# Phases summed in turns in the first four slabs, sixteen more mask matmuls, the last product in two steps, and a new order of the work

## The chip, the core and the metric

The kernel runs on one core of one Trainium2 chip. The metric is device time of one execution in microseconds (us); the time of a kernel is the median of its runs. Engines are named as in the profile: PE multiplies matrices, DVE and ACT do the elementwise work, POOL does next to nothing here, SP starts the DMAs (SPq and ACTq are the queues of SP and ACT).

## What is computed

A linear attention whose state decays by a complex factor, and a gated feed-forward network on its output:

```python
mag = sqrt(a_re**2 + a_im**2)
scale = minimum(mag, 0.999) / (mag + 1e-6)
a_re, a_im = a_re * scale, a_im * scale
for t in range(S):                        # S = 768, for each of B*H = 4*8, D = 48
    S_re, S_im = a_re[t] * S_re - a_im[t] * S_im, a_re[t] * S_im + a_im[t] * S_re
    S_re += k[t] (x) v[t]
    y[t] = q[t] @ S_re
x = y as [3072 tokens, 384]
out = (silu(x @ w_gate) * (x @ w_val)) @ w_out      # 384 -> 1536 -> 384
```

The kernel doesn't step through t. In chunks of 128 rows it sums the logs of the decay's size and its phases from the chunk's first row on, which turns the recurrence into a masked product of q and k with their phases and sizes multiplied in, plus a state that is carried from chunk to chunk.

## The kernel before

**Tiles.** A slab is 128 tokens of one of the four sequences, 8 heads of 48 columns, so 128 by 384. Two slabs make a group g, twelve groups in all; c is the chunk in the sequence that a group belongs to (groups 0 and 1 have c = 0, groups 2 and 3 c = 1, and so on). Group 1 and all later ones treat both slabs in one instruction where they can (128 by 768). Group 0 is the first work of the kernel and is cut in two halves, 0a and 0b, of one slab each.

**Stage of a group** (`stage_ops`). From a_re and a_im come the log of the size (`lnr r0 sqr sqi m2 l2 lnm w`: Ln, Exp, squares) and the phase (`ratio at`: an Arctan). Both are summed over the rows of a chunk by a matmul with the triangular mask `tri`: `cumL` for the log, `cumF` for the phase, one matmul per slab (L545 for groups 0 and 1; L548, with operands in two parts, for later groups). `exps` (L560, L561) takes the exponentials of cumL's sums straight from PSUM. The sums of the phase go through three steps before their cosine and sine are taken:

- `sadd` (L605 to L609) takes the sum from PSUM to SBUF, times 1/(2 pi) (L607), and for c > 0 adds what the chunk before left over (L609, one scalar_tensor_tensor). One instruction per slab.
- `rnd` (L616) rounds that to whole turns, by adding a large constant and taking it away. One instruction per stage.
- `frac` (the helper on L404) subtracts the whole turns. One instruction per stage. What it leaves in the chunk's last row is also stored (`fr`) for the next chunk.

`abs`, `cos` and `sin` (ACT, L453) follow, and the products of q and k with them (`qs0 qs1 ks0 ks1`, DVE, L404).

**Slabs and network.** `slab_ops` transposes (`tr`, L673 for the first four slabs), multiplies q with k (`sc`, L734), masks (`mk`, L762), multiplies with v (`V`, L734), updates the state (`kv`, L800/L803) and copies the result out (`evh`, L821). `ffn_ops` runs twelve blocks f of the hidden width per group: `f1` (L982, both input products), `th` (silu, ACT, L988), `h2` (product, DVE, L993), `hh` and `hl` (high and low part, L408/L410 and L404), `f2` (L1013, the output product, summed over the blocks in PSUM). Then `oe` copies the sums out (L408/L410) and `os` stores them (L1028), in three pieces per group. In group 0 the first four blocks use whole weights and the others weights in two parts; the weights are rounded and split by `c1` to `c5` on DVE and ACT early in the kernel (L873, L408, L410).

**Warm-up and end.** `wm` (L1086) are 48 matmuls of the mask with itself whose result nobody uses; a row of the trace counts each as two passes. `judge`, `tally` (L1040 to L1048) and `keep` (L1052) count how many inputs lie outside the range that this quick way is exact for; after the stores each engine loads the count (L1261) and branches on it (L1262) past `general()`, a slower way that isn't taken with these inputs.

**What sets the order.** The string `ORDER` (L36 on) is the whole order: names of steps, with the engine where there is a choice (`sqi1:ACT`). The planner walks it, puts each step behind the others of its engine, and each engine works its queue in order; a step waits for its operands and for its buffer to come free. Table changes of ACT (L1118) are put in where two neighbours need different tables. DMAs are issued by SP in the same order.

Of the kernel before, what the change touches and what calls it, by code (L numbers as in the profile page):

```python
# [22 lines left out]
P = 128  # L23
# [13 lines left out]
    wm0 wm1 wm2 wm3 wm4 wm5 wm6 wm7 wm8 wm9 wm10 wm11 wm12 wm13 wm14 wm15 wm16 wm17 wm18 wm19 wm20 wm21 wm22  # L37
    wm23 ld_re0a ld_re0b ld_im0a ld_im0b ld_im1 ld_re1 wl00w sqr0a:DVE lnr0a r00a sqi0a:DVE m20a:DVE ld_qt1
    ld_kt0b wl02o wl00o e10a:DVE sqr0b:ACT b10a:DVE lnr0b ld_kt0a r00b ratio0a ld_qt0b lnm0a sqi0b:DVE b10b:DVE
    ldr0 w0a wm24 wm25 wm26 wm27 wm28 wm29 wm30 wm31 wm32 wm33 wm34 wm35 l20a m20b:DVE e10b:DVE at0a cumL0.0  # L40
    wm36 wm37 sqi1:ACT ld_qt0a ldv0 wm38 cumF0.0 sqr1:DVE c10w:DVE m21:DVE lnm0b ratio0b exps0.0 lnr1
    sadd0.0:DVE rnd0a frac0a:DVE lnm1 c30w w1 c10o:DVE dr10a wl02w wl01o r01 l21 w0b wl01w fr0a wl03w b11:DVE
    cumL1.0 e11:DVE ratio1 ldr1 wl03o at0b cumF0.1 l20b abs0a cos0a sin0a qtm0a:DVE ktm0a:DVE at1 cumL0.1
    sadd0.1:DVE dr20a wm39 wm40 wm41 ks0_0a:DVE ks1_0a:DVE trt010 wm42 rnd0b exps0.1 frac0b:DVE wm43 wm44
    exps1.0 dr10b ldv1 qtm0b:DVE abs0b cumF1.0 ktm0b:DVE qs0_0a:DVE qs1_0a:DVE ld_kt1 ld_re2 evt010:ACT cos0b
    wm45 fr0b sadd1.0:DVE wm46 wl04w trt000 cumF1.1 c11w:DVE c31w trt011 wm47 evt000:ACT sadd1.1:DVE sin0b
    trt001 ks0_0b:DVE evt011:ACT cumL1.1 ks1_0b:DVE evt001:ACT qs1_0b:DVE trt110 c12w:DVE qs0_0b:DVE trt111
    wl04o ld_im2 sc0_0 c30o exps1.1 c32w sc1_0 evt110:ACT wl05w dr11 wl08w mk0_0 evt111:ACT trt101 c11o:ACT
    mk1_0 trt100 dr20b evt101:ACT rnd1 frac1:DVE evt100:ACT V0 wl06w c13w:ACT wl07w sc0_1 c31o abs1 wl05o c33w
    sc1_1 mk0_1 wl010w fr1 kv0 evh0 c12o:ACT wl09w mk1_1 c14w:ACT c32o wl06o wl011w V1 gm0 ldv2 c13o:ACT  # L50
    ktm1:DVE kv1 wl08o dr21 evh1 c34w f1_0.0 ldr2 cos1 c33o sin1 qtm1:DVE ks0_1:DVE qs0_1:DVE f1_0.1 c15w:ACT
    ks1_1:DVE th_0.0 round:ACT ld_kt2 h2_0.0 qs1_1:DVE wl07o c14o:ACT trt210 sqr2 c35w f2_0.0 th_0.1 evt210:ACT
    h2_0.1 c16w:ACT c34o trt211 remnant:DVE gm1 trt200 sqi2 evt211:ACT f2_0.1 c36w evt200:ACT trt201 f1_0.2
    m22:DVE c17w:DVE lnm2 c37w evt201:ACT w2 c18w:DVE f1_0.3 c38w lnr2 c15o:ACT r02 c19w:DVE c39w c110w:DVE ldv3
    c310w th_0.3 c35o sc0_2 sc1_2 kv2 th_0.2 ld_qt2 wl09o c111w:ACT h2_0.3 h2_0.2 c16o:ACT b12:DVE trt310 trt311
    c311w evt310:ACT f2_0.2 wl011o c36o e12:DVE c411w:ACT wl010o ldr3 trt300 evt311:ACT f2_0.3 c511w:DVE
    evt300:ACT mk1_2 c410w:ACT c17o:ACT trt301 ratio2 f1_0.4 evt301:ACT c510w:DVE l22 c49w:ACT f1_0.5 c37o
    th_0.4 c59w:DVE c18o:ACT h2_0.4 hs12:ACT c48w:ACT c38o f1_0.6 mk0_2 th_0.5 hh_0.4:ACT c19o:ACT gm2 c58w:DVE
    V2 hl_0.4:DVE h2_0.5 th_0.6 c39o sc0_3 c110o:DVE c310o c111o:DVE c311o hh_0.5:ACT evh2 c47w:ACT sc1_3
    ls12:DVE f1_0.7 c411o:DVE at2 c511o:DVE cumL2.0 c410o:DVE hl_0.5:DVE c510o:DVE h2_0.6 exps2.0 c57w:DVE  # L60
    f2_0.4 f2_0.5 c49o:ACT evl2 hh_0.6:DVE cumL2.1 c59o:DVE f1_0.8 exps2.1 hl_0.6:DVE c46w:DVE c56w:DVE c48o:ACT
    dr12 c58o:DVE ldv4 cy2 f2_0.6 mk1_3 th_0.7 kv3 him2:ACT h2_0.7 mk0_3 dr22 c45w:ACT th_0.8 lim2:DVE f1_0.9
    hh_0.7:ACT c55w:DVE h2_0.8 hl_0.7:DVE V3 c47o:DVE gm3 th_0.9 c44w:ACT c57o:DVE f2_0.7 h2_0.9 c46o:ACT
    c54w:DVE hh_0.9:ACT cumF2.0 evh3 f1_0.10 hl_0.9:DVE c56o:DVE c43w:ACT sadd2.0 c45o:ACT c53w:DVE hh_0.8:ACT
    c55o:DVE cumF2.1 c42w:ACT sadd2.1 hl_0.8:DVE f1_0.11 th_0.10 evl3 rnd2 h2_0.10 f2_0.8 th_0.11 frac2:DVE
    f2_0.9 ldr4 ldr5 ld_im3 fr2 ld_re3 f1_1.0 qtm2:DVE hh_0.10:ACT abs2 c52w:DVE h2_0.11 ktm2:DVE hl_0.10:DVE
# [30 lines left out]
    st8 ls15:DVE hh_3.5:ACT V8 ga8 sh2_9 cumL5.0 hl_3.5:DVE him5:DVE f1_3.7 exps5.0 gm7:DVE gm5:DVE evh8 sh3_9
    cumL5.1 f1_3.8 f2_3.5 exps5.1 evl8 lim5:DVE hh_3.6:ACT sh1_9 dr15 hl_3.6:DVE ld_re6 th_3.7 cumF5.0 th_3.8
    f2_3.6 sadd5.0 h2_3.7 k19 cumF5.1 f1_3.9 kl10 sadd5.1 hh_3.7:DVE os2.0 rnd5 ldr10 frac5:DVE sc0_9 qtm5:DVE
    abs5 sc1_9 h2_3.8 cos5 mk0_9 kv9 fr5 mk1_9 ldv10 st9 ktm5:DVE ld_im6 V9 hl_3.7:DVE qs0_5:DVE th_3.9 k210  # L100
# [1196 lines left out]
```

## Time and profile before

| | |
|---|---|
| median of 3 runs | 610.38 us (609.99 to 611.49) |
| profiled execution: its own time | 611.38 us |
| profiled execution: span, first to last instruction | 609.6 us |
| mean clock granted to PE, of full speed | 0.991 |
| busy PE, DVE, ACT (share of the span) | 594.3 us (97%), 477.2 us (78%), 377.6 us (62%) |

The span is what the trace covers; the profiled execution's own time is 1.78 us longer and lies 1.00 us above the median. Busy shares are means over the whole span. The first 70 us (weights and first stages), the long middle of network blocks and attention interludes, and the last microseconds have different limits and have to be read apart. In a row of the timeline the first number is the start, the second the length from the first instruction's start to the last one's end, and in brackets stands how long the engine had been idle and on what.

### The profile page before, as it was taken

The numbers are of one execution on the slowest core, as the hardware profiler recorded it, in microseconds if no ns is written. First come the engines' busy times: TensorE is split into PE (matmuls) and PEld (weight loads), VectorE is DVE, ScalarE is ACT, GpSimd is POOL, SyncE is SP. The second block draws the span as 40 slices with busy tenths as digits, with TensorE's granted clock in tenths as the row PEclk, the third lists the DMA queues.
The fourth block names the chain that finished last, engine by engine and source line by source line (L and its number), as shares of the span: only waits on it lengthen the run. The fifth ranks groups of instructions, "written<-read, shape, count | busy, mean of one in ns | idle before, by whom it ended". The sixth has DMA issues, their size and how long they took to land.

```text
span 609.6 us, 17179 instructions
## 1 busy us (share of the span) xinstructions
PE 594.3 (97%) x7118; PEld 576.8 (95%) x7118; DVE 477.2 (78%) x893; ACT 377.6 (62%) x664; POOL 5.5 (1%) x17
## 2 busy tenths in 40 slices
PE   7799999999999999999999999999999999999995
PEld 7589999999999999999999999999999999999995
DVE  7999999888869979788879688879685868444442
ACT  7999877676864858839647758647845753212320
POOL 3000000000000000000000000000000000000000
PEclk9799999999999999999999999999999999999998
DMA  8898341654663754656444663656654352262201
GB/s 283 258 369 289 126 80 40 150 150 121 160 160 106 171 141 122 135 140 133 130 102 105 165 153 82 151 159 124 145 151 116 97 163 48 63 164 64 82 24 32
DMA packets 155515, 83.11 MB, mean 136 GB/s; under 512 B 122779, under 2 KB 146589, under 8 KB 155430
## 3 DMA queue, kind: packets, MB, share of 16 engines
q1 hardware_dynamic: 154886, 81.68, 50.5%
q8 instruction: 58, 0.95, 0.7%
q10 hardware_dynamic: 544, 0.26, 0.2%
q14 instruction: 27, 0.22, 0.1%
HBM read 61.40 MB, written 4.78 MB: 109 GB/s over the span
## 4 chain that ended last, share of the span: by engine, by line
PE 86%; DMA 5%; DVE 3%; ACT 2%; SPq 1%; issue 1%; DVEq 0%
PE p_gv L982 45%; PE p_po L1013 23%; PE p_py L734 6%; PE p_ps L734 5%; PE p_pm L548 2%; PE p_pm L803 2%; DMA ww<-in_w_in_dram 2%; DMA wo<-in_w_out_dram 1%; ACT L1118 1%; DMA dec<-dr 1%; DMA ww<-in_a_im_dram 1%; SPq L861 1%; DMA kt<-in_k_dram 1%; DVE ww L404 1%; PE p_gv L545 1%
## 5 line engine op out<-in xcount | busy, mean ns | idle before, releaser
L982 PE MATMUL p_gv<-xh,ww 128*128 128x256 f32 x1728 | 315.4, 280 | 1.0 <-DVE sg L993 0.8
L982 PEld LDWEIGHTS p_gv<-xh,ww 128*128 128x128 f32 x1728 | 270.4, 188 | 2.7 <-DVE sg L993 1.3
L982 PE MATMUL p_gv<-xl,ww 128*128 128x256 f32 x840 | 232.7, 277 | 0.0
L982 PEld LDWEIGHTS p_gv<-xl,ww 128*128 128x128 f32 x840 | 157.7, 188 | 0.0
L1013 PE MATMUL p_po<-hh,wo 128*128 128x256 f32 x840 | 150.6, 279 | 0.0
L988 ACT ACTIVATE sg<-p_gv 128x256 f32<-128x256 f32 x144 | 53.8, 383 | 124.2 <-PE p_gv L982 107.8
L1013 PEld LDWEIGHTS p_po<-hh,wo 128*128 128x128 f32 x840 | 128.1, 188 | 2.4 <-issue 1.8
L1013 PE MATMUL p_po<-hl,wo 128*128 128x256 f32 x420 | 116.5, 277 | 0.2 <-issue 0.2
L1118 ACT ACT_TABLE_LOAD x83 | 106.5, 1283 | 1.4
L993 DVE TENSOR_TENSOR sg<-sg,p_gv 128x256 f32<-128x256 f32 x144 | 59.0, 414 | 51.0 <-ACT sg L988 50.5
L1013 PEld LDWEIGHTS p_po<-hl,wo 128*128 128x128 f32 x420 | 78.8, 188 | 0.4 <-issue 0.4
L404 DVE TENSOR_TENSOR hl<-sg,hh 128x256 fp32r<-128x256 f32 x140 | 57.7, 419 | 12.3 <-ACT hh L408 9.4
L453 ACT ACTIVATE s<-s 128x768 f32<-128x768 f32 x44 | 36.9, 843 | 17.8 <-DVE s L404 7.7
L762 DVE TENSOR_TENSOR sc<-p_ps,turn 128x512 f32<-128x512 f32 x48 | 32.5, 688 | 14.7 <-PE p_ps L734 14.4
L734 PE MATMUL p_ps<-T 96*64 96x128 f32 (+1 forms) x768 | 39.5, 254 | 0.0
L734 PEld LDWEIGHTS p_ps<-T 96*64 96x64 f32 x768 | 36.0, 138 | 3.6 <-issue 1.0
L408 ACT CAST hh<-sg 128x256 fp32r<-128x256 f32 x58 | 23.3, 402 | 23.0 <-PE p_po L1013 16.2
L410 DVE CAST hh<-sg 128x256 fp32r<-128x256 f32 x82 | 23.1, 286 | 6.6 <-PE p_po L1013 4.4
L734 PE MATMUL p_py<-sc,vr 128*32 128x128 f32 x384 | 26.3, 273 | 0.0
L734 PE MATMUL p_py<-sc,vt 128*32 128x128 f32 x384 | 25.2, 273 | 0.1
L734 PE MATMUL p_py<-T,G 96*32 96x128 f32 x640 | 23.4, 279 | 0.0
L921 ACT ACTIVATE wo<-wo 128x384 f32<-128x384 f32 x36 | 20.1, 559 | 5.1 <-DMA wo<-in_w_out_dram 4.1
(133 smaller groups left out, 727.4 us busy)
## 6 DMA issues: line engine op xcount, KB each, us to landing
T<-ww SPq DMA_DIRECT2D x240, 64.0 KB, 2.3
wo<-in_w_in_dram SPq DMA_DIRECT2D x24, 384.0 KB, 4.5
ww<-in_w_in_dram SPq DMA_DIRECT2D x12, 767.8 KB, 7.8
vt<-in_v_dram SPq DMA_DIRECT2D x24, 192.0 KB, 5.3
wo<-in_w_out_dram SPq DMA_DIRECT2D x12, 384.0 KB, 3.1
wo<-in_w_out_dram SPq DMA_DIRECT2D x12, 383.8 KB, 5.6
out_dram<-ost SPq DMA_DIRECT2D x34, 128.0 KB, 4.7
im<-in_a_im_dram SPq DMA_DIRECT2D x11, 384.0 KB, 3.3
```

What stands on the lines that cost most here:

```text
L404: V[e].tensor_tensor(out=out, in0=a, in1=b, op=op)
L408: nc.scalar.copy(out=out, in_=in_)
L410: nc.vector.tensor_copy(out=out, in_=in_)
L453: nc.scalar.activation(out=of(to or dst), in_=of(source), func=func, scale=scale, **kw)
L734: nc.tensor.matmul(out=o, lhsT=l, rhs=r, start=opens, stop=closes, tile_position=(0, width * slot), skip_group_check=True)
L762: nc.vector.tensor_tensor(out=s.rearrange("p (r m) t -> p r m t", m=2), in0=scores[qd].rearrange("p (r m) t -> p r m t", m=2), in1=m, op=A ...
L921: nc.scalar.activation(out=high(0), in_=high(1), func=AF.Square, accum_out=flags[:, fl_hi + j:fl_hi + j + 1])
L982: nc.tensor.matmul(out=gv[:, i, :], lhsT=l, rhs=r, start=(m == 0), stop=(m == len(mm) - 1))
L988: nc.scalar.activation(out=new("sg", I), in_=at_["gv", I][:, 0:2 * P], func=AF.Silu)
L993: nc.vector.tensor_tensor(out=sg, in0=sg, in1=at_["gv", I][:, 2 * P:4 * P], op=ALU.mult)
L1013: nc.tensor.matmul(out=bank(j), lhsT=weight("o", f, part)[:, j * P:j * P + P], rhs=r, start=pos == 0 and m == 0 and j != 1, stop=pos == NF ...
L1118: nc.scalar.preload_act_table_set(op.load)
```

## The change

For c = 0, that is the stages 0a, 0b and 1, `cumF` multiplies with a copy of the mask that is scaled by 1/(2 pi) (`turns`, made on ACT, kept in an output buffer that is free at the start), so that PSUM holds turns. `sadd` falls away there. `rnd` becomes one instruction per slab that reads PSUM and adds the large constant (on DVE, or as an Identity with a bias on ACT, which `rnd1.1` does), `frac` one scalar_tensor_tensor per slab on DVE that takes the constant away again and subtracts the sum in PSUM. The remainder has the other sign; the sine's scale and the subtraction in the next chunk's `sadd` make up for it. The phase sums of group 0 go to the banks of the scores (`ps`), those of the log stay.

Sixteen mask matmuls `wx` may run from `cumF0.0` on, and the cumulating matmuls of 0b stand behind the last of them. The last product of the last group is issued as `f2_11.11` (pieces 0 and 1) and `f3_11.11` (piece 2); of the last three copies two are now ACT's and one DVE's, and of the last stores two are SP's and one ACT's (one and two before). The whole string `ORDER` is written anew: 2217 entries before, 2233 now, about a hundred steps on another engine.

```diff
 ORDER = """
-    wm23 ld_re0a ld_re0b ld_im0a ld_im0b ld_im1 ld_re1 wl00w sqr0a:DVE lnr0a r00a sqi0a:DVE m20a:DVE ld_qt1
-    ld_kt0b wl02o wl00o e10a:DVE sqr0b:ACT b10a:DVE lnr0b ld_kt0a r00b ratio0a ld_qt0b lnm0a sqi0b:DVE b10b:DVE
...
+    wm0 wm1 turns:ACT ld_re0a wm2 ld_im0a wm3 ld_re0b wm4 wm5 ld_im0b wm6 ld_re1 wm7 ld_im1 wm8 wm9 ld_qt0a
+    sqr0a:DVE lnr0a wm10 wm11 wl01w wm12 r00a wm13 wl00w wm14 e10a:DVE wm15 wm16 ld_kt0a wm17 wm18 ldv0
+    sqi0a:ACT wm19 wm20 wm21 ld_kt0b b10a:DVE wm22 wm23 ldr0 wm24 ratio0a wm25 m20a:DVE wm26 at0a sqr1:DVE
...
+    hl_11.11:DVE f2_11.11 f3_11.11 oe11.1 oe11.0 oe11.2 os11.0 os11.2 os11.1
...
+                    if bank == "ps":
+                        at_[bank, inst] = scores[i].rearrange("p h t -> p (h t)")
...
-                        nc.tensor.matmul(out=ps, lhsT=mask, rhs=flat(half(t, i)), start=True, stop=True)
+                        nc.tensor.matmul(out=ps, lhsT=mask if name == "cumL" else at_["ost", "turns"][:, 0:P], rhs=flat(half(t, i)),
+                                         start=True, stop=True)
...
-                elif c == 0:
-                    nc.vector.tensor_scalar(out=s, in0=ps, scalar1=INV_2PI, scalar2=None, op0=ALU.mult)
...
+                ps, u = at_[bank, inst][:, :HD], flat(half("u", i))
+                if e == "ACT":
+                    nc.scalar.activation(out=u, in_=ps, func=AF.Identity, bias=b_magic)
+                else:
+                    nc.vector.tensor_scalar(out=u, in0=ps, scalar1=MAGIC, scalar2=None, op0=ALU.add)
...
+                nc.vector.scalar_tensor_tensor(out=s, in0=u, scalar=MAGIC, in1=ps, op0=ALU.subtract, op1=ALU.subtract)
...
+                nc.vector.scalar_tensor_tensor(out=s, in0=ps, scalar=INV_2PI, in1=s, op0=ALU.mult, op1=ALU.subtract if c == 1 else ALU.add)
...
-        act("sin", "s", "s", AF.Sin, "sin", ["abs", "fr"] if c else ["abs"], scale=-TWO_PI, to=None if c else "sn")
+        act("sin", "s", "s", AF.Sin, "sin", ["abs", "fr"] if c else ["abs"], scale=-TWO_PI if c else TWO_PI, to=None if c else "sn")
...
+            if last:
+                pl.add("f3_" + I, {"PE": 0.34}, lambda e, f2=f2: f2(e, js=(KT - 1,)), deps=["f2_" + I], use=[("hh", I), ("hl", I)] + PO)
...
+            nc.scalar.mul(out=out, in_=mask, mul=INV_2PI)
...
+    for i in range(16):
+        def warm_on(e):
+            nc.tensor.matmul(out=at_["po", "warm"][:, 0:P], lhsT=mask, rhs=mask, start=True, stop=True)
+        pl.add(f"wx{i}", {"PE": 0.225}, warm_on, deps=[f"wx{i - 1}" if i else "cumF0.0", "wm0"], use=[("po", "warm")])
```

What the new order does is seen in the queues. ACT at the start, before: from the table load ahead of `lnm0b` to the Arctan of 0b (L453 are single functions, `s_` and `re` group 1's, `wo_` and `ww_` half-stage 0b's or 0a's):

```order
L1118 ACT_TABLE_LOAD
L453 ACTIVATE wo_93<-wo_93 128x384 [waits DVE_49]
L560 ACTIVATE ww_97<-p_gv 128x8x48 [waits PE_49]
L561 ACTIVATE ww_97,flags<-p_gv 128x8x48
L453 ACTIVATE s_225<-re 128x768 [waits DMAHW5_49]
L453 ACTIVATE s_216<-s_216 128x768 [waits DVE_49]
L453 ACTIVATE s_209<-s_216,b_eps 128x768 [waits Activation_49]
L453 ACTIVATE s_225<-s_225 128x768
L453 ACTIVATE ww_94<-wo_93,b_eps 128x384
L1118 ACT_TABLE_LOAD
L453 ACTIVATE ww_92<-ww_92 128x384 [waits DMAHW3_49,DVE_49]
```

And now, from the table load ahead of the Arctan of 0a on (single functions are L456 here):

```order
L1159 ACT_TABLE_LOAD
L456 ACTIVATE ww_93<-ww_93 128x384 [waits DVE_49]
L1159 ACT_TABLE_LOAD
L456 ACTIVATE wo_94<-wo_94 128x384 [waits DVE_49]
L456 ACTIVATE ww_95<-wo_94,b_eps 128x384 [waits Activation_49]
L456 ACTIVATE s_208<-re 128x768 [waits DMAHW4_49]
...
L568 ACTIVATE ww_98<-p_gv 128x8x48 [waits PE_49]
L569 ACTIVATE ww_98,flags<-p_gv 128x8x48
L456 ACTIVATE s_205<-s_187,b_eps 128x768 [waits Activation_49]
L1159 ACT_TABLE_LOAD
L456 ACTIVATE ww_93<-ww_93 128x384 [waits DMAHW3_49,DVE_49]
```

The first Arctan moved ahead of the size's Ln and Exp, and the functions of 0a, 0b and 1 that need the first table stand in one stretch between the two Arctans.

PE at the start, before: the first cumulating matmuls (`wo_`, `s_` are logs, `ww_`, `im` phases):

```order
L1086 MATMUL p_po<-tri 128x128 x35
L545 MATMUL p_gv<-wo_93,tri 128x384 [waits DVE_49]
L1086 MATMUL p_po<-tri 128x128 x3
L545 MATMUL p_gv<-ww_92,tri 128x384 [waits DMAHW2_49,Activation_49]
L545 MATMUL p_pm<-s_216,tri 128x384 [waits DVE_49]
L545 MATMUL p_gv<-ww_92,tri 128x384 [waits DMAHW3_49,PE_49,Activation_49]
```

And now (L1115 are `wm`, L1129 `wx`, L550 the cumulating matmuls):

```order
L1115 MATMUL p_po<-tri 128x128 x26
L550 MATMUL p_ps_99<-ww_93,ost 128x384 [waits DMAHW1_49,Activation_49]
...
L550 MATMUL p_gv<-wo_94,tri 128x384 [waits DVE_49]
L1129 MATMUL p_po<-tri 128x128 x3
L1115 MATMUL p_po<-tri 128x128 x2
L1129 MATMUL p_po<-tri 128x128 x9
L1115 MATMUL p_po<-tri 128x128 x2
L1129 MATMUL p_po<-tri 128x128
L1115 MATMUL p_po<-tri 128x128 x6
L550 MATMUL p_ps_100<-ww_93,ost 128x384 [waits DMAHW3_49,Activation_49]
```

The phase sum of 0a moved ahead of its log sum; where before two cumulating matmuls stood with nothing between them, a row of mask matmuls now runs up to the phase sum of 0b.

SP at the end, before and now (L1028 and L1056 are the stores, L1261 and L1302 the load of the count, the branch goes past `general()`):

```order
L936 DMA ww_1342<-in_a_im_dram 128x2x384 [waits DMAHW1_49,DVE_49]
L1028 DMA out_dram<-ost 128x2x128 [waits DMAHW0_49,Activation_49]
L1261 TENSOR_LOAD count [waits DVE_49]
L1261 ISA x2
L1262 COMPARE_AND_BRANCH
```

```order
L1302 TENSOR_LOAD count [waits DVE_49]
L1302 ISA x2
L1056 DMA out_dram<-ost 128x2x128 [waits DMAHW0_49,Activation_49]
L1056 DMA out_dram<-ost 128x2x128 [waits DVE_49]
L1303 COMPARE_AND_BRANCH
```

The load of the count moved ahead of the last two stores, and one store came over from ACT's queue.

## Rows read from the trace of the kernel before

**Rows 1.** Stretches of the span: length, busy by engine, granted clock, DMA share, GB/s.

```profile
20.00:25.00 5.00, 5.00 (x18) 3.69 (x17) 4.97 (x12) 4.97 (x12) 0.00 (x0) 0.50 1.01 393
...
40.00:70.00 30.00, 29.86 (x243) 27.33 (x242) 29.76 (x45) 27.62 (x43) 0.00 (x0) 1.00 0.84 281
70.00:590.00 520.00, 518.92 (x6477) 509.73 (x6470) 405.77 (x765) 311.62 (x558) 0.00 (x0) 1.00 0.48 120
```

**Rows 2.** Timeline of PE, 0 to 70 us: start, length, operation, idle before.

```profile
11.90 0.83 PE L1086 MATMUL p_po<-tri 128*128 128x128 f32 x6
12.57 0.81 PE L545 MATMUL p_gv<-ww,tri 128*128 128x384 f32 x2
17.46 0.91 PE L545 MATMUL p_pm<-s,tri 128*128 128x384 f32 x2 [4.08 <-DVE s L517]
19.20 1.65 PE L545 MATMUL p_gv<-ww,tri 128*128 128x384 f32 x2 [0.83 <-ACT ww L453]
...
40.25 1.96 PE L982 MATMUL p_gv<-xh,ww 128*128 128x256 f32 x8
...
66.44 0.80 PE L982 MATMUL p_gv<-xh,ww 128*128 128x256 f32 x2
```

**Rows 3.** Groups of instructions, whole span: steps of the phase.

```profile
L609 DVE SCALAR_TENSOR_TENSOR s<-p_pm,s 128x384 f32<-128x384 f32 x20 | 11.1, 555 | 9.4 <-PE p_pm L548 9.2
...
L616 DVE TENSOR_SCALAR s<-s 128x768 f32<-128x768 f32 x11 | 6.1, 556 | 0.2
...
L404 DVE TENSOR_TENSOR ww<-ww,wo 128x384 f32<-128x384 f32 x2 | 1.1, 559 | 0.1
...
L607 DVE TENSOR_SCALAR s<-p_pm 128x384 f32<-128x384 f32 x2 | 1.1, 552 | 0.5 <-PE p_pm L545 0.5
...
L616 DVE TENSOR_SCALAR wo<-ww 128x384 f32<-128x384 f32 x2 | 0.7, 356 | 0.0
```

**Rows 4.** Timeline of DVE, 0 to 42 us: `sqi0a` and `frac1`.

```profile
5.97 0.62 DVE L404 TENSOR_TENSOR ww<-ww 128x384 f32<-128x384 f32 x1 [2.15 <-DMA ww<-in_a_im_dram]
...
34.14 0.96 DVE L404 TENSOR_TENSOR s<-s,s 128x768 f32<-128x768 f32 x1
```

**Rows 5.** Timeline of ACT, 4 to 20 us: functions and table loads up to the second Arctan.

```profile
4.24 0.51 ACT L473 ACTIVATE wo<-ww 128x384 f32<-128x384 f32 x1
...
12.27 0.52 ACT L453 ACTIVATE wo<-wo 128x384 f32<-128x384 f32 x1
12.70 0.47 ACT L560 ACTIVATE ww<-p_gv 128x384 f32<-128x384 f32 x1
...
13.53 0.84 ACT L453 ACTIVATE s<-re 128x768 f32<-128x768 f32 x1
...
15.14 0.94 ACT L453 ACTIVATE s<-s,b_eps 128x768 f32<-128x768 f32 x1
...
16.71 0.60 ACT L453 ACTIVATE ww<-wo,b_eps 128x384 f32<-128x384 f32 x1
17.33 1.28 ACT L1118 ACT_TABLE_LOAD   x1
18.63 0.52 ACT L453 ACTIVATE ww<-ww 128x384 f32<-128x384 f32 x1
```

**Rows 6.** Timeline, 410.5 to 414 us: the longest wait of PE after 70 us.

```profile
412.96 0.38 PE L982 MATMUL p_gv<-xh,ww 128*128 128x256 f32 x1 [0.81 <-DVE sg L993]
```

**Rows 7.** Timeline of PE, 104.8 to 106 us and 142 to 143 us: two paces of `f1`.

```profile
105.06 0.39 PE L982 MATMUL p_gv<-xh,ww 128*128 128x256 f32 x2
...
105.74 0.39 PE L982 MATMUL p_gv<-xh,ww 128*128 128x256 f32 x2
...
142.14 0.40 PE L982 MATMUL p_gv<-xh,ww 128*128 128x256 f32 x2
...
142.85 0.40 PE L982 MATMUL p_gv<-xh,ww 128*128 128x256 f32 x2
```

**Rows 8.** Timeline, 599 to 610 us: the last stores.

```profile
602.83 0.95 ACTq L1028 DMA_DIRECT2D out_dram<-ost  x2
```

More of the change, by code (lines that the diff above doesn't have):

```diff
@@ L42 @@
[L42 to L66, printed above, removed]
@@ L97 @@
[L97 to L100, printed above, removed]
-    f2_3.7 h2_3.9 evh9 hh_3.9:DVE f1_3.10 ks0_5:DVE hh_3.8:ACT sin5 hl_3.9:DVE k110 sqr6 hl_3.8:DVE kl11 f1_3.11
@@ L444, in load, with act @@
             pl.add(f"ld_{t}{N}", {"SP": 0.49}, fn, deps=[held.get(t, "")], alloc=[tg(t)])
-        def act(name, dst, source, func, table, deps, scale=1.0, bias=None, new_=False, to=None):
+        def act(name, dst, source, func, table, deps, scale=1.0, bias=None, new_=False, to=None, after=()):
             def fn(e):
@@ L610, in stage_ops @@
-            pl.add(f"sadd{g}.{i}", STT1 if c else {"DVE": 0.47, "ACT": 0.376}, total,
-                   deps=[inst, "cy" + N, "e1" + N, "b1" + N] + ([f"sadd{g}.{first}"] if i > first else []),
-                   alloc=[tg("s")] if c == 0 and i == first else [],
-                   use=[(bank, inst)] + ([] if c == 0 and i == first else [tg("s")]))
+                nc.vector.scalar_tensor_tensor(out=s, in0=ps, scalar=INV_2PI, in1=s, op0=ALU.mult, op1=ALU.subtract if c == 1 else ALU.add)
+            if c == 0:
+                pl.add("rnd" + at, {"ACT": 0.52, "DVE": 0.47}, up, deps=[inst] + ([] if g else [f"cumL{g}.{i}"]) + ([] if opens else [f"rnd{g}.{first}"]),
+                       alloc=[tg("u")] if opens else [], use=[(bank, inst)] + ([] if opens else [tg("u")]))
+                pl.add("frac" + at, STT1, rest, deps=["rnd" + at, "e1" + N, "b1" + N] + ([] if opens else [f"frac{g}.{first}"]),
+                       alloc=[tg("s")] if opens else [], use=[(bank, inst), tg("u")] + ([] if opens else [tg("s")]))
+            else:
+                pl.add(f"sadd{g}.{i}", STT1, total, deps=[inst, "cy" + N, "e1" + N, "b1" + N] + ([] if opens else [f"sadd{g}.{first}"]),
+                       use=[(bank, inst), tg("s")])
@@ L615, in rnd @@
         def rnd(e):
             nc.vector.tensor_scalar(out=new(*tg("u")), in0=of("s"), scalar1=MAGIC, scalar2=MAGIC, op0=ALU.add, op1=ALU.subtract)
-        pl.add("rnd" + N, TS, rnd, deps=[f"{x}{g}.{i}" for x in ("sadd", "cumL") for i in slabs], alloc=[tg("u")], use=[tg("s")])
         def frac(e):
             tt(e, of("s"), of("s"), of("u"), ALU.subtract)
-        pl.add("frac" + N, EITHER, frac, deps=["rnd" + N], use=[tg("s"), tg("u")])
+        if c > 0:
+            pl.add("rnd" + N, TS, rnd, deps=[f"{x}{g}.{i}" for x in ("sadd", "cumL") for i in slabs], alloc=[tg("u")], use=[tg("s")])
+            pl.add("frac" + N, EITHER, frac, deps=["rnd" + N], use=[tg("s"), tg("u")])
@@ L622, in stage_ops @@
+        fracs = [f"frac{g}.{i}" for i in slabs] if c == 0 and many > 1 else ["frac" + N]
         if c < NCH - 1:
@@ L1003, in ffn_ops, with f2 @@
                 pl.add("hl_" + I, cost(("DVE", "POOL"), 2 * P), hl, deps=["hh_" + I], alloc=[("hl", I)], use=[("sg", I), ("hh", I)])
-            def f2(e, f=f, I=I, pos=pos, whole=whole):
+            last = g == NGRP - 1 and pos == NF - 1
+            def f2(e, f=f, I=I, pos=pos, whole=whole, js=range(KT - 1) if last else range(KT)):
                 hh, hl, h = (at_.get((x, I)) for x in ("hh", "hl", "sg"))
@@ L1010, in f2 @@
                     new("po", f"{g}.1")
-                for j in range(KT):
+                for j in js:
                     for m, (r, part) in enumerate(products):
@@ L1087, in quick, with in_turns @@
         pl.add(f"wm{i}", {"PE": 0.225}, warm_up, deps=[f"wm{i - 1}"] if i else [], alloc=[] if i else [("po", "warm")], use=[("po", "warm")] if i else [])
+    def in_turns(e):
+        out = new("ost", "turns")[:, 0:P]
+        if e == "ACT":
+            nc.scalar.mul(out=out, in_=mask, mul=INV_2PI)
+        else:
+            nc.vector.tensor_scalar(out=out, in0=mask, scalar1=INV_2PI, scalar2=None, op0=ALU.mult)
+    pl.add("turns", cost(("ACT", "DVE"), P), in_turns, deps=["wm0"], alloc=[("ost", "turns")])
     stage_ops(0, 0, 1)
+    for i in range(16):
+        def warm_on(e):
+            nc.tensor.matmul(out=at_["po", "warm"][:, 0:P], lhsT=mask, rhs=mask, start=True, stop=True)
+        pl.add(f"wx{i}", {"PE": 0.225}, warm_on, deps=[f"wx{i - 1}" if i else "cumF0.0", "wm0"], use=[("po", "warm")])
     stage_ops(0, 1, 1)
```

331 lines of the change are left out of this document (184 added, 147 removed).

## The prediction

> **What bounds the kernel now.** I read the table of stretches first [rows 1]: its columns are PE, PE's weight loads, DVE, ACT, POOL, the granted clock, DMA. The reader is to see two kernels in it. From 70 to 590 us PE is busy for 518.92 of 520 us while DVE has 114 us and ACT 208 us to spare; there only PE's own work, its pace and its few waits count. From 20 to 70 us it is the other way: DVE is busy for 4.97 of 5 and 29.76 of 30 us, ACT for 4.97 and 27.62. PE's busy time says little there, for in the first stretches much of it is mask matmuls that nobody uses. So I went on to PE's timeline [rows 2]. It idles for 4.08 us before 17.46, waiting for DVE, and for 0.83 before 19.20, waiting for ACT's second Arctan. [...] `f1` begins at 40.25 [rows 2]. At 66.44 two of its passes take 0.80 us [rows 2], some 0.4 longer than the pairs around them: there PE has caught up with the weights and casts that DVE and ACT make. After that its waits are few and short.
>
> **The steps of the phase.** Before, the four slabs cost DVE four `sadd` of 0.552, two `rnd` of 0.356 and one of 0.556, two `frac` of 0.559 and one of 0.96 [rows 3, 4]: 2.21 + 1.27 + 2.08 = 5.56 us. Now DVE has three `rnd` that read PSUM and four `frac`. The nearest row for the first is `sadd` itself, one tensor_scalar from PSUM, 0.552; for the second the scalar_tensor_tensor with a PSUM operand, 0.555 [rows 3]: 1.66 + 2.22 = 3.88 us, 1.68 less. ACT gets `rnd1.1`, by the exponential from PSUM 0.47 [rows 5], and `turns`, a third as wide, at most the same: 0.5 to 0.9 more. In 0a and 0b the chain from the sum to the remainder falls from 0.552 + 0.356 + 0.559 = 1.47 to 1.11, 0.36 us a slab.
>
> [...]
>
> **What the new order does to the start.** The time at which 0b's Arctan starts on ACT, 18.63 before [rows 5], is the first thing that moves. The input that `sqi0a` needs is now the second load instead of the third; before, the second load was used at 4.24 [rows 5] and the third at 5.97 [rows 4]. So ACT's square ends near 4.24 + 0.51 = 4.75. Behind it stand up to that Arctan three table loads of 1.28, five functions of 384 columns at 0.52, two with a bias at 0.60, three of 768 columns at 0.84, one with a bias of 0.94, and the two exponentials at 0.47 [rows 5]: 3.84 + 2.60 + 1.20 + 2.52 + 0.94 + 0.94 = 12.04. That gives 16.8, and neighbouring functions overlap by about 0.1 us in the rows while one or two will wait for DVE; I take 16.9, 1.7 us earlier. Bounds: 16.3 if all overlap, 18.6 if DVE's squares, which now take `sqr0b` and `sqi1` over, come late.
>
> **The sixteen mask matmuls.** Three of them run from 11.90 to the start of the next matmul at 12.57 [rows 2], 0.22 us each at full clock: 16 are 3.6 us. They stand in PE's queue between the phase sums of 0a and 0b, where PE idled for 4.91 us before [rows 2], and 14 of the old 48 now stand there as well. The second phase sum can't start before 16.9 + 0.52 = 17.4. The 30 masks take 6.7 us, the log sum between them 0.65 by the distance of the rows; if the first phase sum starts near 9.2 the fillers end at 17.2, so they lie in the wait and cost nothing. If the cover is gone (the Arctan at 16.3), they hold the sum back by 0.4. What they buy is that PE doesn't idle for 4 us before that point. In the trace the lower clock followed right behind such an idle time; I take it that it doesn't fall now.
>
> [...]
>
> **What that is worth.** 0b's chain gains 1.7 at the Arctan, its sums take 0.81 instead of 1.65, and its remainder is 0.36 shorter. But between there and `f1` DVE and ACT had no idle time that could shrink [rows 1], so only a shorter queue counts. DVE saves 1.68; against that `sqr0b` and `sqi1` (0.62 and 0.96 by the same product on DVE [rows 4]) come to it and `sqi0a` (0.62) leaves: 0.96 back. Up to the network's start that is a gain of 0.7 by work, 1.7 by the chain; I take 1.3, `f1` at 38.9 instead of 40.25.
>
> Then most of it is given back. From 40 to 70 us DVE is busy for 29.76 of 30 [rows 1], and up to the high and low parts of the fifth block the new order hands DVE seven casts and one product more and takes one cast from it; at no less than 0.356 each (the cheapest conversion-like row [rows 3]) that is over 2 us, more than the 0.7 that was left. PE, which already caught up at 66.44, comes 1.3 us earlier to weights that are not ready earlier. So it waits there, 0.9 us more in all. ACT is relieved by about as many casts, and has 2.4 us of slack in these 30, so it doesn't add a wait. **Head: -1.3 + 0.9 = -0.4 us**, with -1.7 (all kept, the wait at 66.44 gone too) and +1.1 (the clock falls as before, and DVE's casts come late) as the ends.
>
> **The middle.** The same products in the same number run there, so its sum is 0; but all of its order is new. Two things can shift. A wait such as that at 412.96 (0.81 us [rows 6]) comes or goes with the place of one load or of one DVE step. And the pace: six passes of `f1` start within 0.68 us at one place and within 0.71 at another [rows 7], for whole blocks at a time, with the clock at 1.00 in both. Some three in ten of the stretches that I looked through are of the slower kind, by 4 to 5 ns a pass; for 3800 passes that is near 5 us in which the new order deals the cards again. If that share moves by a third, the time moves by 1.6 us either way. I take 0 and keep -2.5 to +2.5.
>
> **The end.** Before, ACT's queue issued the last two stores in 0.95 us from 602.83 [rows 8], 0.47 each. Now the last store waits for `oe11.2` on ACT, which can start as soon as piece 1 is read, and SP issues two, with its load of the count ahead of them. That load waits only for `keep`, which now stands before the last `h2`, a microsecond earlier. SP's branch comes one issue later (+0.47) but no longer after a load; the last store leaves earlier by about the same. I take 0, ends -0.4 and +0.5.
>
> **Sum.** 0 (masks) - 0.4 (head) + 0 + 0 = -0.4. The profiled execution took 611.38 us, so 611.0 on its scale; it lies 1.00 above the median of 610.38, which gives a median of **610.0 us**.
>
> **Rivals.**
> - *The head's gain is kept and a wait goes.* If DVE's casts are in time, PE comes through 40 to 70 us without a wait (-1.3 and the 0.4 at 66.44), and if the wait at 412.96 goes too that makes -2.5: 607.9 us. For it: PE had one wait only in that stretch. Against: DVE at 99% there. Chance 0.28.
> - *New waits in the middle* (the other side): a load that SP issues late lets DVE's product of `f1`'s two halves come late, and PE, which has no slack, stops as at 412.96, 0.8 us each time. It decides from three such waits on: 610.0 + 2.4 = 612.4 us. For it: every DMA of the middle was moved in SP's queue. Against: the old order has just one such wait in 520 us. Chance 0.14.
> - *The clock falls all the same.* Then the masks don't do what they are there for; sums and transposes of 0b and 1 run at half speed, PE's queue is 1 to 1.5 us late at its 0b sums, and the head's gain is gone: 610.4 to 611.5 us, 611.0 in the middle. For it: the last masks end before the Arctan if that is late. Against: no idle time above 1 us is left. Chance 0.10.
>
> **How the numbers follow.** A measurement of this kernel can tell about 0.3% from no change, 1.83 us: below 608.55 is faster, above 612.21 slower. My forecast has 0.48: its spread comes from the pace and from the ends of the head, about 608.4 to 611.9, so nearly all of it lies within 0.3%, 0.02 on the fast side, 0.02 on the slow. The first rival is faster (0.28), the second slower (0.14), the third the same but for 0.01. Faster 0.30, same 0.53, slower 0.17. The range that leaves out a tenth at either end reaches to the first rival's time and just into the second's: 607.5 to 612.3.
>
> **What would show it.** Right: the granted clock is 1.00 throughout 12 to 40 us and no cumulating matmul takes over 1 us; 0b's Arctan starts at 16.3 to 17.5; `f1` begins at 38.5 to 39.3; PE waits 0.5 to 1.5 us in all between 45 and 65 us for DVE or ACT; seven DVE instructions of 0.55 where ten stood. Wrong: `f1` not earlier than 40 us; a clock of 0.50 anywhere; a wait of more than 0.5 us in PE after 70 us at more than two places; or a share of the slower pace far from three in ten.

## The result, and the profile after

| | before | changed |
|---|---|---|
| median of 18 runs each | 611.22 us (609.36 to 612.96) | 615.30 us (612.37 to 619.32) |
| ratio, 95% interval | | 1.0065 (1.0045 to 1.0084) |
| profiled execution: own time, span | 611.38, 609.6 us | 613.19, 611.3 us |
| mean granted clock | 0.991 | 0.997 |

The change makes the kernel slower by 0.65%, some 4 us. The forecast was 610.0 us, no measurable change, with a range from 607.5 to 612.3. The changed kernel's runs also spread over 7 us, those of before over 3.6; its profiled execution is one of the short ones, 2.1 us under its median.

Stretches of the changed kernel, columns as in [rows 1]:

```profile
20.00:25.00 5.00, 4.60 (x35) 3.33 (x35) 4.90 (x9) 4.97 (x13) 0.00 (x0) 1.00 1.00 289
40.00:70.00 30.00, 27.68 (x227) 24.89 (x225) 27.81 (x43) 26.48 (x39) 0.00 (x0) 1.00 0.85 265
55.00:60.00 5.00, 2.68 (x27) 2.54 (x26) 4.31 (x10) 4.91 (x8) 0.00 (x0) 1.00 0.98 365
70.00:590.00 520.00, 517.27 (x6456) 507.46 (x6455) 404.56 (x764) 308.74 (x557) 0.00 (x0) 1.00 0.49 120
```

The clock stays at 1.00 where it was 0.50. From 40 to 70 us PE has lost 2.2 us of busy time against [rows 1] and DVE, which had no idle time there, 2.0. In the middle PE is busy for 1.65 us less, with the same products to do. The timeline of PE shows the places (second phase sum, first `f1`, then the four longest waits of PE after 30 us):

```profile
18.02 0.81 PE L550 MATMUL p_ps<-ww,ost 128*128 128x384 f32 x2
...
38.19 4.12 PE L1006 MATMUL p_gv<-xh,ww 128*128 128x256 f32 x18
...
58.71 1.08 PE L697 MATMUL p_gv<-ident,ks 128*96 128x128 f32 x8 [2.32 <-DVE sg L1017]
...
214.68 0.39 PE L1039 MATMUL p_po<-hh,wo 128*128 128x256 f32 x1 [0.93 <-issue]
...
266.76 0.27 PE L758 MATMUL p_py<-sc,vt 128*32 128x128 f32 x1 [1.26 <-issue]
...
319.52 0.31 PE L758 MATMUL p_py<-sc,vt 128*32 128x128 f32 x3 [0.43 <-issue]
```

Against [rows 2], `f1` starts 2.06 us earlier. Then 2.32 us go at one place, and three waits follow whose releaser is "issue": the engine waited for nothing that the profile names. Two questions, then: what stops PE near 56 us, and what is behind the three waits by issue.

**The stop near 56 us** can be followed back in the timeline of all engines, in order of time:

```profile
42.22 0.95 DVE L405 TENSOR_TENSOR qs<-qt,re 128x768 f32<-128x768 f32 x1
43.42 0.38 SPq L446 DMA_DIRECT2D re<-in_a_re_dram  x1
...
49.75 0.84 ACT L476 ACTIVATE s<-re 128x768 f32<-128x768 f32 x1 [1.83 <-DMA re<-in_a_re_dram]
...
54.17 0.96 DVE L405 TENSOR_TENSOR re<-re,s 128x768 f32<-128x768 f32 x1 [0.83 <-ACT s L456]
56.42 0.60 DVE L411 CAST xl<-ww 128x768 f16<-128x768 bf16 x1 [0.69 <-DMA ww<-in_w_in_dram]
58.24 0.74 DVE L1017 TENSOR_TENSOR sg<-sg,p_gv 128x256 f32<-128x256 f32 x2
```

The `qs` product reads `re`: the change keeps group 1's rounded turns `u`, and then the cosine in their place, in the buffer of a_re (a line that the diff above leaves out: `at = "re" if t == "u" and g == 1`). So the load of group 2's a_re waits for that product and is issued at 43.42. In the kernel before, SP issued it at 28.72:

```profile
28.72 0.41 SPq L443 DMA_DIRECT2D re<-in_a_re_dram  x1
```

ACT then waits 1.83 us for it, the size's Ln and Exp of group 2 come late and stand ahead of the silu of two blocks, and PE waits for DVE's product `sg`, which follows that silu, to read their sums out of PSUM.

**The waits by issue.** From 212.00 to 213.45 us, just ahead of the first of them, the view of the DMA queues shows one packet of the queue that carries instructions (of 58 in the whole run):

```profile
q8 instruction: 1, 0.02, 5.2%
```

I take these for PE's instructions: the page has 58 packets with 0.95 MB, 16384 bytes each in the trace, and 14300 matmuls and weight loads of PE, so 247 of them to a packet and 66 bytes for one, an estimate from these counts. From 210.30 to 212.80 us PE ran 116 matmuls and 112 weight loads in 2.50 us, from 160 to 170 us 88 and 87 in 10. The theory that follows: where PE runs through many small products it uses its instructions up faster than packets come, and whether it runs dry depends on where the packets' bounds fall in the stream. Sixteen masks are 64 instructions (each is two passes, each with a weight load), by that estimate a quarter of a packet. The rivals: the middle's new order itself; loads that are late from the start on; the masks' work or the clock.

### The profile page after: what moved, and what is told of

It reads as the page before. It is cut to its first block, busy times and chain, and to the rows that moved or that the text cites. A ratio compares the mean times of both kernels' runs of the same rounds, so it can differ in the third digit from the quotient of the medians.

```text
span 611.3 us, 17303 instructions
## 1 busy us (share of the span) xinstructions
PE 596.7 (98%) x7150; PEld 578.6 (95%) x7150; DVE 474.5 (78%) x890; ACT 375.8 (61%) x665; POOL 5.9 (1%) x17
## 4 chain that ended last, share of the span: by engine, by line
PE 86%; DVE 6%; DMA 3%; issue 2%; SPq 1%; ACT 0%; DVEq 0%; ACTq 0%
PE p_gv L1006 46%; PE p_po L1039 24%; PE p_py L758 6%; PE p_ps L758 5%; DMA ww<-in_w_in_dram 3%; PE p_pm L554 2%; PE p_pm L827 2%; DVE ww L405 1%; DMA re<-in_a_re_dram 1%; SPq L583 1%; DVE ww L897 1%; DVE ks L405 1%; DVE wo L897 1%; DVE wo L405 0%; DVE s L405 0%
## 5 line engine op out<-in xcount | busy, mean ns | idle before, releaser
L456 ACT ACTIVATE s<-s 128x768 f32<-128x768 f32 x43 | 36.1, 843 | 16.3 <-DVE s L405 7.8
L409 ACT CAST hh<-sg 128x256 fp32r<-128x256 f32 x59 | 23.7, 404 | 23.0 <-PE p_po L1039 14.7
L845 ACT CAST xh<-p_py 128x384 fp32r<-128x384 f32 x22 | 10.4, 474 | 32.2 <-PE p_py L758 32.2
```

Of the source, the lines that this page charges most:

```text
L409: nc.scalar.copy(out=out, in_=in_)
L456: nc.scalar.activation(out=of(to or dst), in_=of(source), func=func, scale=scale, **kw)
```

## Experiments

Each kernel has 7 to 12 runs beside those of the kernel before, whose median was 611.02 us for experiments 1 to 4, 611.07 for 5, 8, 9 and 10, and 611.39 for 6, 7, 11 and 12. The ratios are to these.

**1. The changed kernel again**, unedited.

> The changed kernel once more, unedited, for a second trace of it; its executions lay between 612.4 and 619.3 us. If its loss sits in the first 70 us (the load of group 2's a_re comes 15 us later in SP's queue, and PE stopped for 2.32 us at 56.15), the same stop is there again, of 2 to 5 us. If it sits in the middle, in waits of PE that the profile puts down to issue (0.93, 1.26 and 0.43 us in the first trace, right behind a packet of PE's instruction queue), they come back at the same three products, with other lengths, 1 to 5 us in all.

614.99 us (612.24 to 617.9), ratio 1.0064 (1.0039 to 1.0089); the profiled execution took 616.41. PE's waits from 70 to 590 us, by what it waited for (total, times, longest):

```profile
PE p_po L1039 <- issue: 1.6, 1, 1.6
PE p_py L758 <- issue: 1.6, 2, 1.1
PE p_po L1039 <- DVE hl L405: 0.4, 1, 0.4
PE p_ps L758 <- issue: 0.3, 1, 0.3
```

The same three products wait, one now for 1.6 instead of 0.93 us, with two smaller ones beside them; the stop near 56 us is there with 2.0 us. The places are the same in both traces; the lengths are not.

**2. The new start with the old middle**, the new end kept:

```diff
-    c41w:ACT h2_1.0 hl_0.11:DVE sin2 qtm2:DVE ks0_2:DVE f2_0.11 th_1.1 c51w:DVE f1_1.2 oe0.0:ACT hh_1.0:DVE
+    c41w:ACT h2_1.0 hl_0.11:DVE sin2 qtm2:DVE ks0_2:DVE f2_0.11 th_1.1 c51w:DVE f1_1.2 ldv5 h2_1.1 hh_1.0:ACT
...
```

> The changed kernel with the order of before from the second product of group 1 on (new steps, new masks, new order of the first 100 us, new end). Theory of the head: the whole loss is here, 613 to 616 us, PE stops near 56 us. Theory of the middle's order: the loss goes, 610 to 611.5 us. Theory of instruction fetches: the sixteen masks shift PE's instructions against the packets in which they come, so waits by issue stand at other places than in before, of 1 to 4 us in all.

610.65 us, ratio 0.9993 (0.9977 to 1.001): the loss is gone, though the stop near 56 us is there (1.8 us). The theory of the head falls as an account of the whole loss. One wait by issue is left in the middle, 0.6 us, below the 1 to 4 that the theory of fetches gave.

**3. The new middle alone**, old start and end:

```diff
-    h2_1.0 h2_1.1 f2_0.11 c51w:DVE hh_1.0:ACT f1_1.2 hl_1.0:DVE ks1_2:DVE qs1_2:DVE hh_1.1:ACT oe0.2:ACT
+    h2_1.0 h2_1.1 f2_0.11 c51w:DVE hh_1.0:ACT sqi3 c43o:DVE f1_1.2 oe0.0:ACT oe0.1:ACT oe0.2:ACT qs0_2:DVE
...
```

> The kernel before with the new order from the second product of group 1 on to the end of group 10 (no new steps, no new masks, old start and end). Theory of the head: as before, 611 us. Theory of the middle's order: 613 to 616 us. Theory of fetches: PE's instructions lie 64 instructions earlier than in the changed kernel, so the three waits by issue are not at the same three products.

609.42 us (608.72 to 610.17), ratio 0.9974 (0.9965 to 0.9984), faster than before. So the middle's order by itself isn't the loss either; the new start, masks included, and the new middle lose only together. One wait of PE is left from 70 to 590 us:

```profile
PE p_ps L734 <- issue: 0.4, 1, 0.4
```

**4. The masks alone**, in the wait of 4.08 us of [rows 2]:

```diff
-    wm36 wm37 sqi1:ACT ld_qt0a ldv0 wm38 cumF0.0 sqr1:DVE c10w:DVE m21:DVE lnm0b ratio0b exps0.0 lnr1
+    wm36 wm37 sqi1:ACT ld_qt0a ldv0 wm38 cumF0.0 wx0 wx1 wx2 wx3 wx4 wx5 wx6 wx7 wx8 wx9 wx10 wx11 wx12 wx13
...
```

> The kernel before with sixteen more mask matmuls alone, in PE's wait of 4.08 us ahead of 17.46; nothing else moved. If the masks only keep the clock up: it stays at 1.00, the cumulating matmuls of 0b take 0.81 instead of 1.65 us, and the time is the same or up to 1 us less, 610 to 611.5. Theory of fetches: the shift of PE's instructions alone changes the waits by issue after 70 us from 0.6 us in all to 1 to 4 us, 611.5 to 614.

610.56 us, ratio 0.9994 (0.9979 to 1.0009), clock at 1.00 throughout, no wait of PE listed from 70 to 590 us. With the old middle the shift does no harm. The forecast of 611.5 to 614 by the theory of fetches missed; the theory stands only if a new place may be as good as the old one.

**5. The new middle and the masks**, experiment 3 with the edit of experiment 4.

> The kernel of the run with the new middle alone (609.42 us), with the sixteen masks added in PE's wait of 4.08 us; so the start of before, the middle's order of the change, and PE's instructions of the middle at the same place of the stream as in the changed kernel. Theory of fetches: the three waits by issue of the changed kernel come back at the same products (an output product near 210 us, products with v near 262 and 315 us), 2.5 to 3.5 us in all, 612 to 613 us. Theory that the loss needs the new start (DMAs that are late from there on): 609 to 609.8, no such waits.

613.98 us, ratio 1.0039 (1.0021 to 1.0056): 4.6 us more than experiment 3, by masks that lie in a wait, and more than the 612 to 613 expected. PE's waits from 70 to 590 us:

```profile
PE p_py L734 <- DVE qs L404: 1.2, 1, 1.2
PE p_py L734 <- issue: 1.0, 1, 1.0
PE p_po L1013 <- issue: 0.8, 1, 0.8
PE p_po L1013 <- DVE hl L404: 0.7, 1, 0.7
```

In its timeline:

```profile
212.90 0.28 PE L1013 MATMUL p_po<-hh,wo 128*128 128x256 f32 x1 [0.76 <-issue]
...
264.39 0.31 PE L734 MATMUL p_py<-sc,vr 128*32 128x128 f32 x3 [1.04 <-issue]
...
298.92 0.39 PE L1013 MATMUL p_po<-hl,wo 128*128 128x256 f32 x1 [0.72 <-DVE hl L404]
...
318.92 0.30 PE L734 MATMUL p_py<-sc,vt 128*32 128x128 f32 x2 [1.24 <-DVE qs L404]
```

An output product at 212.90 us and products with v at 264.39 and 318.92 are the changed kernel's three places, though the profile puts the last down to DVE here. The fourth, at 298.92, waits in experiment 1 too. The start is that of before, so late loads from the new start are not needed for it.

**6. Small matmuls in the masks' place**: experiment 3 with sixteen products of one column by one.

```diff
+            nc.tensor.matmul(out=at_["po", "warm"][0:1, 0:1], lhsT=mask[:, 0:1], rhs=mask[:, 0:1], start=True, stop=True)
...
```

> The kernel with the new middle alone (609.42 us) with sixteen matmuls of one column by one column in the wait of 4.08 us, where the run with masks (613.98 us) had sixteen of 128 by 128: as many instructions in PE's stream, hardly any work, and the clock free to fall as before. Theory of fetches: the waits by issue in products near 210, 262 and 315 us are back, 612.5 to 614.5 us. Theory that the masks' work or the clock makes the loss: 609 to 610 us, no such waits.

614.0 us, ratio 1.0041 (1.0026 to 1.0057). The sixteen take 0.94 us in all, PE idles for 2.77 us behind them, and the granted clock is 0.62 from 15 to 20 us. So neither the masks' work nor the clock makes the loss; the instructions do. PE's waits:

```profile
PE p_py L734 <- issue: 1.6, 1, 1.6
PE p_po L1013 <- issue: 1.1, 1, 1.1
PE p_po L1013 <- DVE hl L404: 0.9, 1, 0.9
PE p_ps L734 <- DMA T<-ww: 0.9, 1, 0.9
PE p_py L734 <- DVE sg L993: 0.5, 1, 0.5
```

**7. Sixty-four of them**, 256 instructions and so about one packet by the estimate above, by the same edit.

> The same with sixty-four of the small matmuls: if each is four instructions of 64 bytes, as the trace counts two passes with a weight load each, that is 16384 bytes, the size of one packet of PE's instruction queue, so the middle's instructions lie against the packets as with none added. Theory of fetches: the waits are gone again, 609.4 to 611 us (the small ones may hold the start up by up to 1 us). If only the number of instructions in the stream counts, not their place against the packets: 613 us or more.

609.71 us, ratio 0.9969 (0.9955 to 0.9984). (The 64 bytes of the expectation are an assumption near the estimate of 66.) Four times as many instructions, and the loss is gone; PE's only wait from 70 to 590 us:

```profile
PE p_ps L736 <- DMA T<-ww: 0.6, 1, 0.6
```

So the number of instructions alone doesn't make the loss: sixteen more lose 4.6 us, sixty-four more nothing.

**8. The changed kernel without the new masks.**

```diff
-    for i in range(16):
-        def warm_on(e):
...
```

> The changed kernel without the sixteen new masks (wx), all else as it is. Theory of fetches: the three waits by issue go, 2.5 to 3.5 us less than the changed kernel, 611.5 to 612.5 us; the stop near 56 us stays at about 2 us. Theory that the start's late DMAs make all of the loss: 614.5 to 616 us, or more if the clock falls. If the masks are what keeps the clock up, a stretch with a granted clock of 0.50 shows between 15 and 30 us.

611.12 us, ratio 0.9989 (0.9975 to 1.0004): 3.9 us less than experiment 1. The waits in the middle are gone but for 0.2 us, the stop near 56 us is still there (2.8 us), and the clock falls as in [rows 1]. From 20 to 25 us:

```profile
20.00:25.00 5.00, 5.00 (x21) 4.30 (x21) 4.90 (x9) 3.75 (x10) 0.00 (x0) 0.50 0.86 222
```

So with the masks the clock stays up, and `f1` starts 1.6 us later without them (39.75); that is worth less than what they shift.

**9. The buffer of u moved**, and the load of group 2's a_re put back to an earlier place in SP's order (`ld_re2`, not shown).

```diff
+    W["w", 11] = place("w", 11, F32)
+    fixed["lent", "u1", 0] = W["w", 11][:, 0:A2].rearrange("p (h d) -> p h d", d=D), ("w", 11)
...
-            at = "re" if t == "u" and g == 1 else LATER.get(t, t)
+            at = ("lent", "u1", 0) if t == "u" and g == 1 else LATER.get(t, t)
```

> The changed kernel with one buffer moved: the rounded turns u of group 1 lie in space that is lent from a weight tile that is loaded late, not in the buffer of a_re; so the load of group 2's a_re no longer waits for the last product that reads u (DVE, to 43.2 us), and it is put where before had it in SP's queue, some 15 us earlier. Theory of the head: ACT's wait of 1.8 us for that load goes, PE's stop near 56 us falls from 2.0 to 2.3 us to under 0.7, 1.5 to 2.5 us less than the changed kernel, 612.5 to 613.5 us. If the stop comes from the weights (the load of the eleventh weight tile, for which DVE waited 0.69 us): the stop stays above 1.5 us, 614.5 to 615.5.

614.48 us, 0.5 less than experiment 1, which is within the spread of the two. Neither case of the expectation came: the stop goes and the time hardly does. The load is issued at 27.35, the stop near 56 us is gone, and a shorter one stands for it at 46.39 (DVE waits for another DMA):

```profile
46.39 0.64 PE L699 MATMUL p_gv<-ident,ks 128*96 128x128 f32 x4 [0.81 <-DVE sg L1019]
```

The three waits of the middle are all there (0.93, 1.32 and 0.39 us in its trace).

**10. Both edits**, experiments 8 and 9.

> Both edits: the buffer of u moved and no new masks. If the two causes are separate and are all of the loss, it gains both: 609 to 610.5 us. If it also keeps the earlier start of the network (38.2 instead of 40.3 us): down to 607.5. If one of the two causes is wrong: 612 or more.

610.18 us, ratio 0.9977 (0.9963 to 0.9991), 0.9 less than experiment 8 and 4.3 less than experiment 9. It is as fast as expected, but not by an earlier start: the first group's last output product ends at 99.55 us in its trace, at 98.88 in that of before.

**11. Experiment 9 with forty-eight small matmuls behind the last new mask**, so that masks and small ones make one packet.

> The changed kernel with the buffer of u moved (614.48 us), its masks kept, and forty-eight of the small matmuls behind the last new mask: with the sixteen masks that makes one whole packet. Theory of fetches: the waits by issue near 213, 265 and 319 us go, 3 to 4 us less, 609 to 611 us; the clock stays at 1.00. Rival, more instructions make more waits: 614 or more.

611.75 us, ratio 1.0004 (0.9988 to 1.002): 2.7 less than experiment 9, short of the 3 to 4 expected. The waits are gone (one of 0.4 us is listed from 70 to 590 us), but the small ones and the masks behind them hold the second phase sum up to 21.30 us, where experiment 9 has it at 17.42, and the granted clock is 0.66 from 20 to 25 us: `f1` starts at 41.43.

**12. The new end on experiment 3** (last product in two steps, copies, stores and load of the count as in the change).

> The start of before (old steps, no new masks) with the new middle and the new end (last product in two steps, two of the last copies on ACT, two last stores on SP, count loaded ahead of them): the parts of the change without its start. From the last product to the end of the span the old end took 7.1 to 7.9 us in the traces so far, the new one 6.7 to 7.3. If the new end is worth that 0.5 us: 608.7 to 609.2 us; if not, 609.4.

609.37 us, ratio 0.9968 (0.9955 to 0.998), the same as experiment 3. The new end is worth nothing that can be measured. Experiments 3, 7 and 12 beat both kernels, by 1.6 to 2.0 us against before: the best that this change holds is its order of the middle, with PE's instructions left where they were.

| start | middle | PE's instructions shifted by | median, us |
|---|---|---|---|
| old | old | 0 | 611.22 |
| old | old | 16 masks | 610.56 |
| new | old | 16 masks | 610.65 |
| old | new | 0 | 609.42 |
| old | new | 16 masks, 16 small ones | 613.98, 614.00 |
| old | new | 64 small ones | 609.71 |
| new | new | 16 masks | 614.99, 615.30 |
| new | new | 0 | 611.12 |

The loss of 3.9 to 4.6 us comes with a shift of a quarter packet and only with the new middle. With the buffer of u moved it is the same: 614.48 with sixteen masks, 610.18 with none, 611.75 with a whole packet.

**Where the waits stand.** The traces say more about the theory. Count PE's instructions by start (matmuls, weight loads, those of its sequencer). The three products that wait in the changed kernel and in experiments 1, 5, 6 and 9 are then always numbers 4801, 6081 and 7617, give or take one: 1280 and 1536 apart, five and six times 256. One packet of 16384 bytes for every 256 instructions makes 64 bytes for one, an estimate from these two numbers; the counts of the page gave 66. The waits of `p_py` by issue in experiments 2, 8, 10 and 11 stand on the same grid (4801, 6337, 4033, 4289), and so do the two short ones by issue in the kernel before (0.16 us at 8386, 0.11 at 11201). So I take these for the bounds between packets. The short waits of `p_ps` in experiments 1, 3 and 9 are not: that product waits for a DMA in experiments 6, 7 and 12. For number 4801, with packets and bounds paired in order:

| trace | packet starts, us | 4801 starts, us | between, us | PE idle before it, us |
|---|---|---|---|---|
| before | 211.32 | 216.61 | 5.29 | 0 |
| experiment 3 | 212.02 | 216.41 | 4.39 | 0 |
| experiment 4 | 210.51 | 212.85 | 2.34 | 0 |
| experiment 2 | 214.34 | 216.76 | 2.42 | 0.55 |
| changed | 212.11 | 214.68 | 2.57 | 0.93 |
| experiment 5 | 210.31 | 212.90 | 2.59 | 0.76 |
| experiment 6 | 211.93 | 214.59 | 2.66 | 1.10 |
| experiment 1 | 214.11 | 217.01 | 2.90 | 1.64 |

In all fourteen traces nothing behind a bound starts less than 2.18 us after its packet does, and every wait of more than 0.15 us at a bound ends 2.2 to 2.9 us after it. Where PE's other work brings it to the bound later than that, as before and in experiment 3, nothing is lost. The shift of 64 instructions decides which products lie at a bound. It accounts for most of the loss: product by product, experiment 5's trace falls behind experiment 3's by 0.92, 1.25 and 1.41 us around the three bounds, by 1.09 around the wait at 298.92, and by nothing from 332 us on.

## Why the prediction was wrong

Of the 5.3 us between 610.0 and 615.30, 0.84 lie in the kernel before, whose median was 610.38 in the three runs of the forecast and 611.22 in the eighteen of the result. The change itself was forecast at -0.4 us and measured at +4.1. An estimate of its parts: the new middle -1.6 (experiment 3), the shift of PE's instructions +4.6 (experiment 5 against 3), the start +1.0 (the later end of the first group, below).

The first point rests on two rows of the changed kernel, the Arctan of 0b on ACT and the instruction of DVE that reads its phase sum:

```profile
16.30 0.52 ACT L456 ACTIVATE ww<-ww 128x384 f32<-128x384 f32 x1
...
21.49 0.55 DVE L616 TENSOR_SCALAR wo<-p_ps 128x384 f32<-128x384 f32 x1
```

- **The masks.** Their own time cost nothing, though they filled more than the wait. The second phase sum started at 18.02, 1.2 us behind the Arctan's end (the bound given was 0.4), because the first one came at 10.03 and not near 9.2. But DVE, busy with other work, took the sum up at 21.49 only. The clock stayed up as forecast (1.00 in the stretches from 12 to 25 us); in experiment 8, without them, it was 0.50 from 20 to 25 us. In the kernel before it was 1.00 up to 18 us and 0.68 from 18 to 19, right behind the wait that ended at 17.46. The step that failed is the sentence that the masks "lie in the wait and cost nothing", the term 0 of the sum. They also move every later instruction of PE against the packets, and with the new middle that costs 4.6 us (experiments 3, 5, 6 and 7). The text priced time on PE's queue and never the stream that feeds it.
- **The middle.** "I take 0" failed with it. The second rival named new waits in the middle, but as loads that come late, and priced 2.4 us. The waits are there, at the bounds of packets. Without the shift the new middle is 1.6 us faster than the old one, inside the range of -2.5 to +2.5 that was given for it. The pace did no harm: passes of `f1` and `f2` from 70 to 590 us start 114.50 ns apart on the mean before and 114.31 in the changed kernel (distances under 130 ns), some 0.7 us less in 3800.
- **The start.** The Arctan of 0b came at 16.30 (forecast 16.9, lower bound 16.3), `f1` at 38.19 (38.9). "Most of it is given back" was right in sign, and 0.9 us too small by far: the first group's last output product ends at 99.92, 1.04 us later than before, so 3.1 us were given back. The mechanism was another. The text looked at DVE's casts and not at which buffer `u` now lies in, so the 14.7 us by which a load was put off had no term. With that buffer moved (experiment 9) the first group ends 0.17 us before the old kernel's, where the forecast had -0.4.
- **The steps of the phase** cost what the nearest rows said: 0.553 and 0.551 for `rnd`, 0.552 and 0.549 for `frac`; `rnd1.1` on ACT took 0.58 instead of 0.47. **The end** at 0 was right (experiment 12).
- The slower side of the range ended at 612.3. It had bounds for clock, pace and waits, and none for a resource that the trace of before hardly showed: its own waits by issue came to less than 0.3 us there.

What is shown is that the loss comes and goes with the shift, with a period that a whole packet fits, and that PE waits at the bounds of packets. Two things stay open. No run shows why a packet starts when it does (58 instructions ahead of number 4801 in the changed kernel, 172 ahead before). And the wait at 298.92, number 6904, isn't at a bound; what delays DVE there wasn't followed.

## What to carry to other kernels

Here filler instructions in a wait of PE shifted all that followed them: with the new middle sixteen cost 4.6 us (experiments 5 and 6 against 3) and sixty-four nothing (experiment 7). So a change that adds some should be timed with a second number of them. Where a buffer gets a second tenant, look up which DMA waits for it to come free, and where in its queue that DMA now stands: here it was issued at 43.42 instead of 28.72 us. Waits that the profile puts down to issue are worth listing by place before and after a change. Here their places, counted in PE's instructions, differed by multiples of 256, and that is what pointed to the packets.

## What the runs showed of the hardware

- PE waits for 0.4 to 1.6 us each, at instructions whose numbers differ by multiples of 256, and goes on 2.2 to 2.9 us after the start of a packet of the instruction queue (the changed kernel and experiments 1, 2, 5, 6, 9, 10 and 11). The 58 packets in the trace of the changed kernel have 16384 bytes each. The lists of waits from 70 to 590 us show none at such a number in experiments 3, 4 and 7; experiments 1, 5 and 6, where they stand, are 3.9 to 4.6 us slower than the same kernel without the shift (experiments 8, 3 and 3).
- The changed kernel's 18 runs reach from 612.4 to 619.3 us, experiment 3's 11 from 608.7 to 610.2. That the waits make this spread was not tested; their lengths differ between the two traces of the changed kernel (0.93 and 1.64 us at the same product).
- In experiment 7 PE ran sixty-four products of one column by one for 3.34 us and idled for 0.37 us behind them; the granted clock was 0.78 from 15 to 20 us and 0.54 from 20 to 25. In experiment 4, with sixteen masks of 128 by 128 in that place, it was 1.00 in both.
